# Dealing the first group's weight steps out earlier in a fused retention and feed-forward kernel

## The chip, the cores and the metric

One core of one Trainium2 chip runs the whole kernel. The metric is the device time of one execution in microseconds; the kernel before was run three times, and one further execution was profiled.

## The reference, cut to what matters

Attention with decay (retention) over 4 batches, 8 heads, 576 positions and a head size of 64; then two feed-forward layers over the 2304 tokens of 512 channels, with 2048 hidden units each.

```python
scores = scale * np.matmul(q, k.transpose(0, 1, 3, 2))
ret = scores * Dmat[None, :, :, :]      # gamma_h ** (i - j) for i >= j, else 0
x = np.matmul(ret, v)                   # -> tokens x 512
h = x @ w_in;  x = np.maximum(0.01 * h, h) @ w_out
h = np.maximum(x @ w_in2, 0.0);  x = h * h @ w_out2
```

The weights reach the chip as 64-bit floats, read as pairs of 32-bit words. Products are made of three passes of a high and a low part each, so every weight and every operand is split on the chip into a "hi" and a "lo" tile.

## The kernel before, in words

**Attention stage.** 20 chunks, 0 to 19: five a batch, four of 128 tokens and one of 64. For a chunk i of the loop (L611) the program issues the loads of chunk i + 4 on the SP queue, then `scores` and `decay` of chunk i + 2, then `output` of chunk i. `scores` (L501) is 16 matmuls on PE into one of two wide PSUM tiles, and a product with the mask on DVE into r (L513). So PE can't begin the scores of chunk i + 2 until DVE has made r of chunk i. `decay` (L515) is up to two products on GpSimd (POOL). `output` (L528) is r times v (L539), q times the running state (L542), the sums for the next state (L548) on PE; ACT copies the sums into the state (L554) and the output into ysb (L557). Every engine takes its instructions in the order in which the program issues them.

**Weight steps.** Dealt out between the chunks are two lists of other work. `Weights.steps` is a generator that turns weights into hi and lo tiles, one step each time it is asked. A group of hidden units has four weights, two input weights with 12 steps each (L151) and two output weights with 8 each (L191): 40 steps, of which most are one DVE instruction. Steps 1, 13, 25 and 33 begin a weight with the exponent on ACT (L149). Steps 10, 11, 22 and 23 have the hi copies of input weights on ACT (L185), followed by the lo of DVE (L187). Of an output weight, the first step also holds the shift at L201, and then come L203, L205, L207, L209 on DVE, the hi on ACT (L212), and L214 and L216 on DVE. All weights pass through one tile `raw` and one work tile `sf`. `RATE[i]` says how many steps follow the output of chunk i; `FIRST` runs three before chunk 0; `run` stops at `GROUP - OWN`, 40 less `OWN`; and what is missing to this count is run in one go after the last chunk (L651). When the weight in hand no longer needs `raw`, `next` (L137) sets `free`, and the following chunk issues the next load (L617), up to four loads (`GRP`) in this stage. After the stage a load is issued by `next` itself. A step whose weight has not been asked for yields, and the caller goes on without it.

**Operand builds.** `operands(0, 0)` makes the seven operands x of the first 768 tokens out of ysb, in eleven steps behind chunks 8 to 18 (`BUILD`): hi on ACT (L256), lo on DVE (L260), sums on DVE (L270 to L281). The x tiles are also stored to DRAM by SP (L237) for later groups.

**Feed-forward stage.** Two layers, four groups each, three pairs of token blocks p each. `first` (L334) makes seven products (L318) by Strassen's scheme into two wide PSUM tiles a and b, in the order A11, A12, S2, S3, S1, A22, S4; the first two of the whole stage are issued early, behind chunks 17 and 18 (L639). The sum at L370 reads b, and PE can write S3 into b only after it; the sum at L384 reads a, which S4 then overwrites. `second` (L402) is the products with the output weights (L419). `pace` (L665) asks for weight steps between these, up to a share of the group's 40 that `SHARE` gives by the place reached, at most two a call.

Of the kernel before, what the change touches and what calls it, by code (L numbers as in the profile page):

```python
# [23 lines left out]
GRP = 4  # L24
# [6 lines left out]
HW = DM // 2  # L31
SLOTS = 7
INS, OUTS = 3, 2 * NU
RATE = [1, 2, 2, 2] + [2] * 6 + [1, 1, 2, 2, 2, 0, 0, 0, 1, 2]
BUILD = [0] * 8 + [1] * 11 + [0]
DEEP = 4
SPACE = .65
SHARE = {0: (0.15, 0.45), NG - 1: (0.47, 0.85), NG: (0.2, 0.55)}
OWN = 5
LAG = 1  # L40
ARRIVE = 3
FIRST = 3
# [8 lines left out]
def retention_ffn_kernel(ctx: ExitStack, tc: tile.TileContext, full, rows, half, halfv, w1, w2, const, mask, gk, out):  # L51
# [44 lines left out]
    def weight_tiles(pool, ins, outs):  # L96
        for _ in range(ins):
            i = len(in_tiles)
            in_tiles.append((pool, i))
        for _ in range(outs):  # L100
            i = len(out_tiles)
            out_tiles.append((pool, i))
# [139 lines left out]
    def operands(layer, p):  # L242

        x = ysb[p].rearrange("p (k t n) -> p k t n", k=NK, t=2)
        b11, b21, b12, b22 = (x[:, k : k + 2, t] for t in range(2) for k in (0, 2))
        t2 = stage.tile([P, 2, HT], F32, tag="t2", name="t2")

        xt = {}

        def hi(i, src):  # L250
            use = layer, 0, p, i
            while uses[loaded[0]] != use or loaded[0] == used[0] + SLOTS:
                yield True
            loaded[0] += 1
            xt[i] = xs[use] = xpool.tile([P, 2, 2, HT], F32R, tag="x", name="x")
            nc.scalar.activation(xt[i][:, 0], src, AF.Copy)  # L256

        def lo(i, src):
            t = xt[i]
            nc.vector.tensor_tensor(t[:, 1], src, f32(t[:, 0]), sub)  # L260
            kept.append(((layer, 0, p, i), t))


        yield from hi(0, b11)
        yield
        yield from hi(1, b21)
        lo(0, b11)
        yield
        lo(1, b21)
        nc.vector.tensor_tensor(b11, b12, b11, sub)  # L270
        yield
        nc.vector.tensor_tensor(t2, b22, b11, sub)
        yield
        yield from hi(2, t2)
        nc.vector.tensor_tensor(b12, b22, b12, sub)
        yield
        yield from hi(3, b12)
        lo(2, t2)
        yield
        yield from hi(4, b11)  # L280
        nc.vector.tensor_tensor(b21, b21, t2, sub)  # L281
        yield
        yield from hi(5, b21)
        lo(3, b12)
        yield
        yield from hi(6, b22)
        lo(4, b11)
        yield
        lo(5, b21)
        yield  # L290
        lo(6, b22)
        yield
# [267 lines left out]
    weights = Weights()  # L560
# [5 lines left out]
    def run(n, limit):  # L566

        while n > 0 and done[0] < limit:
            if next(steps, None):
                break  # L570
            done[0] += 1
            n -= 1

    def build(n=1):

        ran = 0
        while builds and ran < n:
            try:
                if next(builds[0]):
                    break  # L580
                ran += 1
            except StopIteration:
                builds.pop(0)
        return ran

    GROUP = NU * (STEPS_IN + STEPS_OUT)
    with tc.manual_schedule():
        with tc.tile_pool(name="att", bufs=1) as pool:
# [22 lines left out]
            for i in range(n):  # L611
# [16 lines left out]
                if a < 2 * HT <= a + t:  # L628
                    builds.append(operands(0, 0))
                run(min(1, RATE[i]), GROUP - OWN)  # L630
                if BUILD[i] > 0:
                    build()
                run(RATE[i] - 1, GROUP - OWN)
                if BUILD[i] > 1:
# [8 lines left out]
                    else:  # L643
                        early.append(sums1)
        att.clear()
        if weights.free and weights.loads < GRP:
            weights.ahead()
        more = ctx.enter_context(tc.tile_pool(name="more", bufs=1))
        gp = ctx.enter_context(tc.tile_pool(name="gp", bufs=1))
        weight_tiles(more, INS - NU, OUTS - NU)  # L650
        run(GROUP, GROUP - OWN)  # L651
        weights.arrive = ARRIVE
# [110 lines left out]
```

## Time and profile before

| | us |
|---|---|
| median of 3 runs | 845.59 |
| lowest and highest | 843.33, 846.24 |
| the profiled execution | 844.29 |
| its span in the trace | 842.5 |
| PE busy in the span | 824.2 (98%) |
| DVE, ACT, POOL busy | 601.4, 340.7, 49.8 |

Rows of the trace give the start of an instruction or of a run of like ones, in us from the start of the span, then the time, the engine, the line and the tiles written and read; in brackets is how long the engine sat idle before it and what released it. The mean granted TensorE clock of the span is 0.993 of full speed.

### The profile page before, as it was taken

Reading aid. Unit: us, or ns where it says so; the run is one execution under the profiler, and the core shown is the slowest. Engines: PE = TensorE matmul, PEld = TensorE weight load, DVE = VectorE, ACT = ScalarE, POOL = GpSimd, SP = SyncE. Lnnn points to the kernel's source line nnn. Section 1 sums busy time; section 2 is a strip of 40 time slices with the busy share of each in tenths; the row PEclk is TensorE's granted clock in tenths of the full one; section 3 lists DMA queues with packets and bytes.
Section 4 is the critical chain, followed back from the end, with each engine's and each line's share of the span. In section 5 each row is a group of like instructions: output and inputs, shape, how many; then the busy total and the mean of one; then the engine's idle time right before and its main releaser. Section 6 shows DMA issues by size and latency. Waiting matters only on the chain.

```text
span 842.5 us, 12378 instructions
## 1 busy us (share of the span) xinstructions
PE 824.2 (98%) x5084; PEld 778.0 (92%) x5084; DVE 601.4 (71%) x734; ACT 340.7 (40%) x447; POOL 49.8 (6%) x36
## 2 busy tenths in 40 slices
PE   6999999999999999999999999999999999999998
PEld 6878899999999999999999998988998998998996
DVE  4799588758667576658667879868777778754534
ACT  1455557545424424424425365543322333321211
POOL 3766000000000000000000000000000000000000
PEclk8999999999999999999999999999999999999999
DMA  9998463967547647646832554966755646735711
GB/s 334 346 311 288 181 241 95 420 264 279 217 190 268 219 150 298 242 147 242 301 112 103 209 226 163 368 255 238 285 183 206 262 160 252 262 133 204 286 52 75
DMA packets 45688, 191.01 MB, mean 227 GB/s; under 512 B 5696, under 2 KB 6720, under 8 KB 45632
## 3 DMA queue, kind: packets, MB, share of 16 engines
q1 hardware_dynamic: 45632, 190.22, 60.7%
q8 instruction: 40, 0.66, 0.3%
q14 instruction: 16, 0.13, 0.0%
HBM read 152.45 MB, written 37.75 MB: 226 GB/s over the span
## 4 chain that ended last, share of the span: by engine, by line
PE 86%; DVE 7%; DMA 4%; ACT 1%; issue 1%; SPq 0%; DVEq 0%; ACTq 0%
PE yps L419 46%; PE a L318 22%; PE b L318 16%; DMA raw<-in_w 1%; DVE r L513 1%; DMA x<-x 1%; DVE x L260 1%; PE scps L511 1%; DMA kt<-in_full 1%; DMA kv<-in_rows 1%; PE ops L539 1%; PE ops L542 1%; DVE sf L205 1%; ACT sf L149 1%; DVE ilo L187 1%
## 5 line engine op out<-in xcount | busy, mean ns | idle before, releaser
L318 PE MATMUL a<-x,ihi 128*128 128x384 f32 x768 | 196.0, 336 | 2.2 <-DVE t L384 2.1
L318 PE MATMUL b<-x,ihi 128*128 128x384 f32 x576 | 147.2, 336 | 2.1 <-DVE t L370 2.1
L318 PEld LDWEIGHTS a<-x,ihi 128*128 128x128 f32 x768 | 138.9, 188 | 4.3 <-DVE t L384 3.4
L419 PE MATMUL yps<-ghi,ohi 128*128 128x384 f32 x384 | 128.6, 335 | 0.6 <-ACT ysb L428 0.6
L318 PE MATMUL a<-x,ilo 128*128 128x384 f32 x384 | 128.6, 335 | 0.0
L419 PE MATMUL yps<-ghi,olo 128*128 128x384 f32 x384 | 128.3, 334 | 0.0
L419 PE MATMUL yps<-glo,ohi 128*128 128x384 f32 x384 | 128.3, 334 | 0.0
L356 DVE TENSOR_TENSOR glo<-t,ghi 128x768 fp32r<-128x768 f32 x96 | 91.7, 955 | 45.8 <-ACT ghi L351 45.3
L430 DVE TENSOR_TENSOR ysb<-yps,ysb 128x384 f32<-128x384 f32 (+1 forms) x126 | 76.0, 610 | 62.6 <-PE yps L419 62.1
L419 PE MATMUL yps<-ohi,glo 128*128 128x512 f32 x288 | 112.3, 390 | 0.0
L419 PE MATMUL yps<-olo,ghi 128*128 128x512 f32 x288 | 112.3, 390 | 0.0
L419 PE MATMUL yps<-ohi,ghi 128*128 128x512 f32 x288 | 112.0, 389 | 0.0
L351 ACT ACTIVATE ghi<-t 128x768 fp32r<-128x768 f32 x96 | 81.1, 845 | 68.5 <-DVE t L329 55.1
L318 PEld LDWEIGHTS b<-x,ihi 128*128 128x128 f32 x576 | 104.3, 189 | 2.6 <-DVE t L370 2.4
L344 ACT ACTIVATE s<-a 128x768 f32<-128x768 f32 x47 | 38.2, 813 | 157.3 <-PE a L318 157.2
L318 PE MATMUL b<-x,ilo 128*128 128x384 f32 x288 | 96.8, 336 | 0.0
L419 PEld LDWEIGHTS yps<-ghi,ohi 128*128 128x128 f32 x384 | 72.1, 188 | 1.5 <-ACT ysb L428 0.9
L318 PEld LDWEIGHTS a<-x,ilo 128*128 128x128 f32 x384 | 72.2, 188 | 0.0
L419 PEld LDWEIGHTS yps<-glo,ohi 128*128 128x128 f32 x384 | 72.1, 188 | 0.0
L419 PEld LDWEIGHTS yps<-ghi,olo 128*128 128x128 f32 x384 | 72.1, 188 | 0.0
L419 PEld LDWEIGHTS yps<-ohi,glo 128*128 128x128 f32 x288 | 54.1, 188 | 11.2
L419 PEld LDWEIGHTS yps<-olo,ghi 128*128 128x128 f32 x288 | 54.1, 188 | 11.0
(67 smaller groups left out, 1002.5 us busy)
## 6 DMA issues: line engine op xcount, KB each, us to landing
x<-x SPq DMA_DIRECT2D x168, 768.0 KB, 6.2
raw<-in_w SPq DMA_DIRECT2D x62, 512.0 KB, 5.1
kv<-in_rows SPq DMA_DIRECT2D x16, 512.0 KB, 6.2
out<-ysb SPq DMA_DIRECT2D x18, 256.0 KB, 2.0
q<-in_full SPq DMA_DIRECT2D x16, 256.0 KB, 5.8
kt<-in_full SPq DMA_DIRECT2D x16, 256.0 KB, 5.6
ysb<-in_w SPq DMA_DIRECT2D x2, 512.0 KB, 7.1
gq<-in_const SPq DMA_DIRECT2D x3, 256.0 KB, 7.3
```

What stands on the lines that cost most here:

```text
L149: nc.scalar.activation(f32(a), f32(raw[:, :, 1]), AF.Abs)
L187: nc.vector.tensor_tensor(lo[:, a:z], sf[:, a + 1 : z + 1], f32(hi[:, a:z]), sub)
L205: nc.vector.scalar_tensor_tensor(rest, high, 23, low, ALU.logical_shift_left, ALU.bitwise_or)
L260: nc.vector.tensor_tensor(t[:, 1], src, f32(t[:, 0]), sub)
L318: nc.tensor.matmul(ps[:, u, :HT], a[:, w, s], x[:, b, k], start=(start and k == 0 and i == 0), stop=(k == 1 and i == 2), skip_group_check= ...
L344: nc.scalar.activation(t, ps[:, :, :HT], AF.Copy)
L351: nc.scalar.activation(h, t, AF.Copy)
L356: nc.vector.tensor_tensor(l, t, f32(gs[key][0]), sub)
L419: nc.tensor.matmul(acc, a, b, start=(j == u == i == 0), stop=(j == 1 and u == NU - 1 and i == 2))
L430: nc.vector.tensor_tensor(y, acc, y, add)
L511: nc.tensor.matmul(ps[:n, j, p, :n], k[s, c], q[s, c], start=True, stop=True)
L513: nc.vector.tensor_tensor(t[:n, :, :, :n], ps[:n, :, :, :n], self.mask[:n, :, :, :n], mul)
```

## The change

The first group's steps are dealt out at another rate: three a chunk from chunk 2 to chunk 7, two a chunk from 8 to 11, one behind chunk 12, none behind chunks 13 to 17, two behind 18 and three behind 19. `OWN` falls from 5 to 2, so that up to 38 of the 40 steps may run in the attention stage. Since `next` of the fourth weight then falls in this stage, the load after it, the next group's first, is issued right behind the last chunk.

```diff
-RATE = [1, 2, 2, 2] + [2] * 6 + [1, 1, 2, 2, 2, 0, 0, 0, 1, 2]
+RATE = [1, 2] + [3] * 6 + [2] * 4 + [1] + [0] * 5 + [2, 3]
 BUILD = [0] * 8 + [1] * 11 + [0]
...
-OWN = 5
+OWN = 2
...
         att.clear()
-        if weights.free and weights.loads < GRP:
+        if weights.free:
             weights.ahead()
```

## Rows read from the trace of the kernel before

**Rows 1.** Windows: busy us of PE, PEld, DVE, ACT, POOL; clock, DMA share, GB/s.

```profile
36.00:60.00 24.00, 23.00 (x362) 20.24 (x358) 22.45 (x21) 12.87 (x25) 17.53 (x14) 1.00 0.89 308
93.00:97.00 4.00, 4.00 (x16) 4.00 (x15) 2.49 (x4) 3.56 (x5) 0.00 (x0) 0.57 0.37 113
```

**Rows 2.** Waits of PE, 17 to 92 us: total us, times, longest.

```profile
PE scps L511 <- DVE r L513: 2.2, 4, 0.9
```

**Rows 3.** Timeline of PE: start us, us, line, tiles, count, idle before, releaser.

```profile
59.09 1.16 PE L542 MATMUL ops<-q,state 128*128 128x128 f32 x8
...
61.72 1.16 PE L511 MATMUL scps<-q,kt 64*128 64x128 f32 x16 [0.86 <-DVE r L513]
...
71.27 1.16 PE L511 MATMUL scps<-q,kt 64*128 64x128 f32 x16 [0.33 <-DVE r L513]
...
74.25 1.13 PE L542 MATMUL ops<-q,state 128*128 128x128 f32 x8 [0.80 <-POOL kv L526]
...
79.26 0.62 PE L318 MATMUL a<-x,ihi 128*128 128x384 f32 x2
...
92.50 0.61 PE L318 MATMUL b<-x,ihi 128*128 128x384 f32 x2 [2.08 <-DVE t L370]
...
132.77 0.61 PE L318 MATMUL a<-x,ihi 128*128 128x384 f32 x2 [0.98 <-DVE t L384]
```

**Rows 4.** Chain of waits, 92 to 101 us: start us, us, engine, tile, line.

```profile
92.50 3.53 PE b L318 x12
96.04 2.46 PE a L318 x12
98.50 2.08 PE b L318 x12
```

**Rows 5.** Timeline of DVE, columns as in rows 3.

```profile
30.29 0.41 DVE L179 TENSOR_TENSOR sf<-sf 128x256 f32<-128x256 f32 x1
32.09 1.23 DVE L513 TENSOR_TENSOR r<-scps,mask 128x1024 f32<-128x1024 f32 x1 [1.39 <-PE scps L511]
33.23 1.05 DVE L187 TENSOR_TENSOR ilo<-sf,ihi 128x768 fp32r<-128x768 f32 x1
35.08 1.23 DVE L187 TENSOR_TENSOR ilo<-sf,ihi 128x1024 fp32r<-128x1024 f32 x1 [0.80 <-ACT ihi L185]
...
38.85 1.38 DVE L159 TENSOR_SCALAR sf<-sf 128x1024 f32<-128x1024 f32 x1 [1.41 <-ACT sf L149]
...
49.11 1.38 DVE L175 TENSOR_TENSOR sf<-sf 128x256 f32<-128x256 f32 x1
...
56.19 1.21 DVE L513 TENSOR_TENSOR r<-scps,mask 128x1024 f32<-128x1024 f32 x1
57.32 0.94 DVE L187 TENSOR_TENSOR ilo<-sf,ihi 128x768 fp32r<-128x768 f32 x1
...
61.59 1.21 DVE L187 TENSOR_TENSOR ilo<-sf,ihi 128x1024 fp32r<-128x1024 f32 x1
...
64.20 0.67 DVE L201 TENSOR_SCALAR raw<-raw 128x1024 uint32<-128x1024 uint32 x1
...
67.40 1.20 DVE L205 SCALAR_TENSOR_TENSOR sf<-raw 128x1024 uint32<-128x1024 uint32 x1
...
70.00 1.21 DVE L513 TENSOR_TENSOR r<-scps,mask 128x1024 f32<-128x1024 f32 x1
```

**Rows 6.** Timeline of ACT, columns as in rows 3.

```profile
88.60 1.12 ACT L149 ACTIVATE sf<-raw 128x1024 f32<-128x1024 f32 x1
...
104.82 1.57 ACT L256 ACTIVATE x<-ysb 128x768 fp32r<-128x768 f32 x2
```

**Rows 7.** DMA issues (KB each, median us to landing); then SP's timeline.

```profile
x<-x SPq DMA_DIRECT2D x168, 768.0 KB, 6.2
...
kt<-in_full SPq DMA_DIRECT2D x16, 256.0 KB, 5.6
...
72.40 0.81 SPq L132 DMA_DIRECT2D raw<-in_w  x2
```

## The prediction

> **What bounds the kernel now.** I went from the windows to PE's waits, then to what DVE, ACT and POOL did under them. Chunks are counted 0 to 19; the first group's weight steps 1 to 40 (1 to 12 and 13 to 24 for the two input weights, 25 to 32 and 33 to 40 for the third and fourth, which are output weights). The attention stage ends where the first early product starts on PE, at 79.26 us [rows 3]; until then DVE and PE are both nearly full [rows 1], and what PE waits for is mostly the masked scores r that DVE makes: 2.2 us in four waits [rows 2], two of them in [rows 3], with one more of 0.80 at 74.25. The profile books that one to POOL, but the code gives L542 the state, which ACT copies right behind the hi of step 30 (L212), itself waiting for DVE's L209; I take it as the price of an ACT step that waits for DVE ahead of the state copy. Then comes the largest single wait of PE, 2.08 us before the product at 92.50, for the sum at L370. Its cause stands on ACT: the fourth weights' exponent (L149, step 33) starts only at 88.60, behind the last chunk's copies [rows 6], and L203, L205 and L370 queue behind it on DVE. After that wait PE is granted 0.57 of its clock [rows 1], so it spends most of that stretch at the lower of its two levels, 1.2 GHz: two products of twelve matmuls take 3.53 and 2.46 where the next takes 2.08 [rows 4], so the clock costs 1.45 + 0.38 = 1.83 us more. Behind it PE runs to the end with few waits, so what moves PE here by some us moves the end by as much.
>
> **What the edit does, counted.** Before, 4 steps are run by the end of chunk 0, 6 by chunk 1, then two a chunk: 22 by chunk 9, 28 by chunk 13, 33 by chunk 19 and 35 before the feed-forward stage. After, 9 by chunk 2, 12, 15, 18, 21, 24 by chunk 7, then 26, 28, 30, 32, and 33 by chunk 12; none until chunk 18 runs two and chunk 19 three: 38. By this count step 33, the exponent that starts late, runs in chunk 12, and five steps, not six, lie behind the last two chunks. Up to chunk 1 nothing changes; from the second pair of products of the feed-forward stage on (p = 1) the steps are asked for by the same table, so only the time between changes. The work in all is the same.
>
> **Gain at L370.** With step 33 done in chunk 12, L207 and L209 are all that precedes L370 after the last chunk and they wait for no ACT instruction; the sum's inputs are there while PE is busy with S2. So the 2.08 goes. With PE unbroken I expect no fall of the clock, which takes the 1.83 too: -3.91 us. Bounds: at most that; at the least 2.08 minus what is late next, which is the hi of step 38 (L212) at the place on ACT where L149 stood, with nothing on DVE ahead of L370 behind it.
>
> **Loss before it: r of chunk 12.** r(12) is queued on DVE behind the steps of all chunks up to 9: 22 before, 28 after. The six added are L187 twice, L201, L203, L205, L207: 0.94 + 1.21 + 0.67 + 0.67 + 1.20 + 0.67 = 5.36 [rows 5] (L201 stands there for L203 and L207, of the same kind and shape), less about 0.07 each, by which one starts ahead of the former's end (56.19 + 1.21 against 57.32): 4.94 us. Against it stands idle time of DVE that they fill: 1.39 + 0.80 + 1.41 = 3.60 before [rows 5]. Not all of it can be used: steps 11 and 12 now stand in chunk 3 ahead of r(6), and step 11 needs ACT's hi, which needs chunk 3's copies. DVE is done by 30.29 + 0.41 less the overlap, 30.63, and the lo at L187 starts no sooner than its row, 33.23: 2.60 us of idle, with r(6) stuck behind it and the second lo until about 35.3 instead of 32.09. So 1.0 us is regained, and r(12) starts at 56.19 + 4.94 - 1.0 = 60.1.
>
> From there to the end of the stage: step 29 (L209) and step 30 (L212) now follow r(12), as they follow the r at 70.00 before, and from that r's start to the L542 that waited for the state copy the rows give 74.25 - 70.00 = 4.25. From chunk 12's L542 (59.09) to the early product (79.26) PE took 20.17, of which 0.86 + 0.33 + 0.80 were waits [rows 3]: 18.18 unbroken. Behind chunk 12 DVE has hardly a step left, so I let those waits go. The early product starts at 60.1 + 4.25 + 18.18 = 82.5: **+3.3 us**. Bounds: below, PE cannot do better than without its waits, 2.2 + 0.8 = 3.0 us sooner; above, every added step can meet a POOL instruction as the L175 at 49.11 did, 1.38 against 0.41 for an instruction of that shape [rows 5], 0.97 each: 6 x 0.97 = 5.8 more, +9.1. I take +3.3 since POOL has the same instructions as before.
>
> That price rests on a collision which the rows show for instructions with two SBUF inputs and not for r, 1.21 at 56.19 as at 70.00. [...]
>
> **Smaller terms.** Steps 39 and 40 and five of the next group's, which ran behind the first products' matmuls at L419, now fall among the first seven products, and L384 is queued behind L161 and L163. PE waited 0.98 for an L384 so placed at 132.77 [rows 3]. Between 0 and 1.0 I take 0.5.
> On SP the second output weight's load moves from chunk 15 to chunk 11 and has the loads of chunks 16 to 19 behind it; it waits for step 29. That ends about 60.1 + 2 x 1.13 = 62.4, after which kt of chunk 16 is issued near 63.7 and lands 5.6 later [rows 7], 69.3. PE wants it 5.6 us of matmuls after L542(12), at about 70: covered by 0.7 us, and a rival below if not. The third weight's load moves two chunks up and is covered by chunk 7's work. The next group's first load moves ahead of the six stores of x on SP and waits for step 37. Their slots are written again from 104.82 [rows 6]; 1 MB and six times 768 KB [rows 7] at 308 GB/s [rows 1] take about 18.5 us from about 88, and the slots come up one by one, the first after 6 us: nothing.
>
> **Sum.** -3.91 + 3.3 + 0.5 = -0.1 us. The profiled execution took 844.29 us, its span 842.5 and 1.8 around it, so 844.2; it stands 1.3 below the median of the runs shown, 845.59, on which the sum gives **845.5**. 0.3% is 2.5 us, about what a measurement can tell from no change.
>
> **Rivals**, by where r(12) starts (each us later is a us at the end):
> 1. *The early steps stay hidden.* If collisions become fewer since the steps spread over more of POOL's idle time, and r(12) starts by 57.7, the stage loses under 0.9 and the net is below -2.5. At the floor, 3.0 sooner: -3.91 - 3.0 + 0.5 = -6.4, 839.2; midway 841. For it: DVE idles 3.60 in [rows 5], and DVE has slack again from chunk 13. Against: the order on DVE puts two of the steps on an ACT round trip. 27%.
> 2. *Collisions multiply (slower).* Denser steps meet POOL in chunks 4 to 9, and r(12) starts after 62.8, a net above +2.5. Three more of 0.97 give 848.4; all six 851.3. It would also lengthen PE's single waits, and one near 2 us could lower the clock again, as at 92.50. For it: POOL is busy 17.53 of the 24 us [rows 1]. Against: POOL's count is unchanged. 20%.
> 3. *Chunk 16's kt is late (slower).* The load on SP that waits for step 29 keeps it. The 1 MB ahead of it at 308 GB/s is 3.4 us, less the 0.7 of cover: up to 2.7, so 848.2. No such wait is in the rows, where the attention loads are all issued before the second output weight's, at 72.40 [rows 7]. 4%.
> 4. *The steps don't move*, because a load is not yet asked for and the generator yields: then the catch-up run in front of the feed-forward stage takes them, and the time stays 845.6. The count above speaks against it. 3%.
> The forecast itself has 46%, its own range 843 to 848.
>
> **Numbers.** Faster by over 0.3%: 27%, rival 1. Slower: 20 + 4 = 24%. Within: 46 + 3 = 49%. The range, 840.5 to 849.5, takes most of rival 1 and all but the dense end of rival 2.
>
> **What would show it.** Right: no PE wait at L370 and a granted clock near 1.00 behind S2; the first early product 2 to 5 us after 79.26; PE waits for r of chunks 6 to 12 and one before chunk 12's L542; none from chunk 13 on. The first step: r(6) near 35.3 instead of 32.09. The second: r(12) near 60. Wrong: an early product at or ahead of 79.26 (rival 1), one behind 85 or short matmuls at the lower clock in that stage (rival 2), a PE wait for a DMA of kt (rival 3), or a difference behind 160 us, which no step here explains.

## The result: slower by 0.57%, and the profile after

The changed kernel took **849.03 us** (median of 5 runs, 848.18 to 850.09), the kernel before 844.27 (5 runs beside them): a ratio of 1.0057, 95% interval 1.0040 to 1.0073. The forecast was 845.5, no change to be told. The range, 840.5 to 849.5, held the time, but that is partly luck: it was built on the 845.59 of the three runs shown. On 844.27 the forecast change of -0.1 gives 844.2 and the same range ends at 848.2, below what was measured. The likeliest case and its chance were wrong: rival 2, which had 20%, came true. The profiled execution took 848.18 us, the lowest of the five, with a span of 846.4, 3.9 more than that of before; the medians are 4.8 apart. PE is busy as long as before (824.3 us against 824.2): in sum, what was added is waiting.

(PE is the matrix engine, DVE the vector engine, ACT the scalar engine, POOL is GpSimd, and SP issues the loads.)

The windows of the changed kernel, for the stretches of [rows 1] (busy us of PE, PEld, DVE, ACT and POOL, then clock, DMA share, GB/s):

```profile
36.00:60.00 24.00, 20.36 (x304) 17.86 (x302) 22.75 (x23) 12.49 (x23) 13.68 (x10) 0.93 0.78 267
93.00:97.00 4.00, 4.00 (x39) 3.68 (x38) 1.34 (x2) 1.75 (x3) 0.00 (x0) 1.00 0.90 296
```

From 36 to 60 us PE now works 20.36 us instead of 23.00 and its clock is at 0.93; around the old wait at L370 it is full and at 1.00. So the loss lies ahead of the early products and the gain behind. The waits of PE from 17 to 110 us, against [rows 2], show with whom:

```profile
PE scps L511 <- DVE r L513: 6.2, 5, 2.0
PE ops L542 <- ACT state L554: 1.3, 1, 1.3
PE a L318 <- DVE t L384: 0.7, 1, 0.7
```

6.2 us for r instead of 2.2. The timeline of PE, with the columns and places of [rows 3]:

```profile
38.01 1.16 PE L511 MATMUL scps<-q,kt 64*128 64x128 f32 x16 [1.18 <-DVE r L513]
...
42.38 0.68 PE L511 MATMUL scps<-q,kt 64*64 64x64 f32 x16 [0.48 <-DVE r L513]
...
47.77 1.16 PE L511 MATMUL scps<-q,kt 64*128 64x128 f32 x16 [1.98 <-DVE r L513]
48.86 1.62 PE L539 MATMUL ops<-r,kv 128*64 128x128 f32 x16
50.41 2.08 PE L542 MATMUL ops<-q,state 128*128 128x128 f32 x8
...
64.28 0.68 PE L511 MATMUL scps<-q,kt 64*64 64x64 f32 x16 [1.93 <-DVE r L513]
...
67.26 1.13 PE L542 MATMUL ops<-q,state 128*128 128x128 f32 x8 [1.27 <-ACT state L554]
...
69.67 1.16 PE L511 MATMUL scps<-q,kt 64*128 64x128 f32 x16 [0.67 <-DVE r L513]
...
86.18 0.62 PE L318 MATMUL a<-x,ihi 128*128 128x384 f32 x2
...
97.19 0.51 PE L318 MATMUL b<-x,ihi 128*128 128x384 f32 x2
...
104.33 0.62 PE L318 MATMUL a<-x,ihi 128*128 128x384 f32 x2 [0.73 <-DVE t L384]
...
106.55 0.33 PE L419 MATMUL yps<-ghi,ohi 128*128 128x384 f32 x1
```

The early product starts at 86.18 instead of 79.26. Behind the wait of 1.98 us two runs of matmuls take 1.62 and 2.08 instead of their usual 1.09 and 1.16: the lower clock (0.56 is granted from 48.86 to 52.42), where the kernel before was granted 1.00 from 36 to 60 [rows 1]. The wait at L370 is gone (S3 goes on at 97.19 without a gap), and there is one of 0.73 at L384.

The timeline of DVE, which answers to [rows 5]:

```profile
24.40 1.23 DVE L513 TENSOR_TENSOR r<-scps,mask 128x1024 f32<-128x1024 f32 x1 [1.47 <-PE scps L511]
...
33.78 3.04 DVE L187 TENSOR_TENSOR ilo<-sf,ihi 128x768 fp32r<-128x768 f32 x2 [1.68 <-ACT ihi L185]
36.74 1.21 DVE L513 TENSOR_TENSOR r<-scps,mask 128x1024 f32<-128x1024 f32 x1
...
44.63 1.95 DVE L168 SCALAR_TENSOR_TENSOR sf<-raw,sf 128x1024 f32<-128x1024 uint32 x1
...
55.78 0.69 DVE L203 TENSOR_SCALAR sf<-sf 128x1024 f32<-128x1024 f32 x1 [1.01 <-ACT sf L149]
...
57.52 2.17 DVE L205 SCALAR_TENSOR_TENSOR sf<-raw 128x1024 uint32<-128x1024 uint32 x1
59.62 1.79 DVE L260 TENSOR_TENSOR x<-ysb,x 128x768 fp32r<-128x768 f32 x1
...
61.33 1.76 DVE L207 TENSOR_SCALAR sf<-sf 128x1024 uint32<-128x1024 uint32 x1
63.01 1.21 DVE L513 TENSOR_TENSOR r<-scps,mask 128x1024 f32<-128x1024 f32 x1
```

r of chunk 6 is at 36.74 instead of 32.09, r of chunk 12 at 63.01 instead of 56.19. L205, L260 and L207, which take 1.22, 0.95 and 0.69 us where GpSimd's products are left out (below), take 2.17, 1.79 and 1.76.

One thing has to be taken off before the sum: the r of chunk 3, the last one ahead of anything the change moves, starts at 24.40, in the kernel before at 23.84:

```profile
23.84 1.23 DVE L513 TENSOR_TENSOR r<-scps,mask 128x1024 f32<-128x1024 f32 x1 [1.70 <-PE scps L511]
...
102.50 0.33 PE L419 MATMUL yps<-ghi,ohi 128*128 128x384 f32 x1
```

These 0.56 us belong to the start of that one execution: over all sixteen profiles of this document the r of chunk 3 starts anywhere from 22.48 to 25.92, with either table. The rest, by places:

| us, from the trace | before | after | difference |
|---|---|---|---|
| r of chunk 3 | 23.84 | 24.40 | +0.56, not of the change |
| from there to r of chunk 12 | 32.35 | 38.61 | +6.26 |
| from there to the early product | 23.07 | 23.17 | +0.10 |
| from there to the first L419 | 23.24 | 20.37 | -2.87 |
| from there to the end of the span | 740.00 | 739.85 | -0.15 |
| span | 842.5 | 846.4 | +3.9 |

The first L419 is the second line above. From there on the two kernels are alike. The stretch from r of chunk 3 to r of chunk 12 hardly varies: it is 38.59 to 38.87 us in the five profiles below and above that have the new table up to chunk 11 and GpSimd's products, and 32.35 to 32.60 in the eight that have the old one. So the +6.26 is the change's, not one execution's.

### The profile page after: what moved, and what is told of

It is laid out like the page before. It is cut to its first block, busy times and chain, and to the rows that moved or that the text cites. A ratio compares the mean times of both kernels' runs of the same rounds, so it can differ in the third digit from the quotient of the medians.

```text
span 846.4 us, 12380 instructions
## 1 busy us (share of the span) xinstructions
PE 824.3 (97%) x5084; PEld 777.6 (92%) x5084; DVE 604.9 (71%) x734; ACT 340.2 (40%) x447; POOL 47.5 (6%) x36
## 4 chain that ended last, share of the span: by engine, by line
PE 88%; DVE 5%; DMA 4%; ACT 2%; issue 1%; SPq 0%; DVEq 0%; ACTq 0%
PE yps L419 46%; PE a L318 22%; PE b L318 16%; DMA kt<-in_full 2%; PE ops L542 1%; PE ops L539 1%; PE scps L511 1%; DMA raw<-in_w 1%; DMA kv<-in_rows 1%; ACT sf L149 1%; DVE ilo L187 1%; PE sums L548 1%; DVE r L513 1%; DVE sf L205 1%; DVE t L370 0%
## 5 line engine op out<-in xcount | busy, mean ns | idle before, releaser
L419 PE MATMUL yps<-ghi,ohi 128*128 128x384 f32 x384 | 128.6, 335 | 0.5 <-ACT ysb L428 0.4
L419 PE MATMUL yps<-ghi,olo 128*128 128x384 f32 x384 | 128.3, 334 | 0.0
L419 PE MATMUL yps<-glo,ohi 128*128 128x384 f32 x384 | 128.3, 334 | 0.0
L419 PE MATMUL yps<-ohi,glo 128*128 128x512 f32 x288 | 112.3, 390 | 0.0
L419 PE MATMUL yps<-olo,ghi 128*128 128x512 f32 x288 | 112.2, 390 | 0.0
L419 PE MATMUL yps<-ohi,ghi 128*128 128x512 f32 x288 | 112.0, 389 | 0.0
L344 ACT ACTIVATE s<-a 128x768 f32<-128x768 f32 x47 | 38.3, 814 | 157.0 <-PE a L318 156.9
L419 PEld LDWEIGHTS yps<-ghi,ohi 128*128 128x128 f32 x384 | 72.1, 188 | 1.4 <-ACT ysb L428 0.8
L419 PEld LDWEIGHTS yps<-glo,ohi 128*128 128x128 f32 x384 | 72.1, 188 | 0.0
L419 PEld LDWEIGHTS yps<-ghi,olo 128*128 128x128 f32 x384 | 72.1, 188 | 0.0
L370 DVE TENSOR_TENSOR t<-b,s 128x768 f32<-128x768 f32 x24 | 23.0, 957 | 61.8 <-PE b L318 57.2
L419 PEld LDWEIGHTS yps<-ohi,glo 128*128 128x128 f32 x288 | 54.0, 188 | 11.3
```

What stands on the lines that cost most here:

```text
L344: nc.scalar.activation(t, ps[:, :, :HT], AF.Copy)
L370: nc.vector.tensor_tensor(t11, b[:, :, :HT], s1, add)
L419: nc.tensor.matmul(acc, a, b, start=(j == u == i == 0), stop=(j == 1 and u == NU - 1 and i == 2))
```

## Experiments

Times are medians. "Before" stands for the kernel before, run beside each of them: 844.2 to 844.4 us.

**Loss and gain taken apart.** First the late half alone, then the early half alone.

```diff
# late half alone, on the changed kernel
-RATE = [1, 2] + [3] * 6 + [2] * 4 + [1] + [0] * 5 + [2, 3]
+RATE = [1, 2, 2, 2] + [2] * 6 + [1, 1, 2, 2, 2, 1, 1, 1, 2, 3]
# early half alone, on the kernel before (OWN = 5)
-RATE = [1, 2, 2, 2] + [2] * 6 + [1, 1, 2, 2, 2, 0, 0, 0, 1, 2]
+RATE = [1, 2] + [3] * 6 + [2] * 4 + [0] * 7 + [1]
```

> The changed kernel's OWN of 2 and early load, but the five steps added to the kernel before's table stand behind chunks 15 to 19 instead of 2 to 12. Theory (the loss is the steps put ahead of r in chunks 2 to 9, the gain is step 33 off the end): the early product starts within 1 us of the 79.26 of before, no wait at L370, 2.08 + 1.83 gained less about 0.7 at L384: 841 us. Rival (the wait at L370 vanished only because PE came 7 us later): the wait is still there and the time is that of before, 844.3.

> The changed kernel's table up to chunk 11, but step 33 behind the last chunk and OWN of 5, as before. Theory (loss and gain are separate): the early product near 86, as in the changed kernel, and the wait of about 2 us at L370 with the lower clock behind it back again: 844.3 + 6.9 = 851 us. Rival (the late PE hides that wait anyway): 849, as the changed kernel.

The early half alone came out near the theory: 850.52 us (four executions), ratio 1.0065 (1.0044 to 1.0087). That is above the whole change, but the intervals overlap; the trace decides. Its early product starts at 87.43, and the wait at L370 is back:

```profile
100.66 0.62 PE L318 MATMUL b<-x,ihi 128*128 128x384 f32 x2 [2.08 <-DVE t L370]
```

The lower clock that I expected behind it did not come back. The window from 100.60 to 106.00 us, with the columns of [rows 1]:

```profile
100.60:106.00 5.40, 5.34 (x31) 5.34 (x31) 3.88 (x6) 3.92 (x5) 0.00 (x0) 1.00 0.46 127
```

So the loss sits in the early steps, and the gain at L370 is separate from it. The late half alone missed: 845.5 us, ratio 1.0014 (1.0000 to 1.0027), where I expected 841. Its executions fall into two groups, 843 to 845 and 846 to 848, and the profiled one, 847.59, is of the upper: there PE waits 2.85 us for the r of chunk 16, ahead of which the steps are those of the kernel before, and 1.26 at L384, where ACT waits 0.69 for the early load. The wait of 2.85, and the last of the three DVE instructions ahead of that r:

```profile
75.19 2.08 PE L511 MATMUL scps<-q,kt 64*128 64x128 f32 x16 [2.85 <-DVE r L513]
...
72.26 1.75 DVE L207 TENSOR_SCALAR sf<-sf 128x1024 uint32<-128x1024 uint32 x1
```

and GpSimd at the same place in the kernel before:

```profile
66.85 4.37 POOL L522 TENSOR_TENSOR q<-q,gq 128x512 f32<-128x512 f32 x1 [5.41 <-PE scps L511]
```

In the kernel before L205, L260 and L207 run there in 1.20, 0.94 and 0.68 us and GpSimd's product is the one that gets longer; here they take 1.52, 1.79 and 1.75. It is the same meeting, and the other engine loses it. What decides that, and whether it is what makes the two groups, was not settled. That the late half has a cost of its own is followed up below.

**GpSimd's part.** Its decay products were taken out of both kernels.

```diff
     def decay(self, i):
         q, _, kv = self.raw[i]
...
-            if c > 0:
-                q = q[:, : NP * n].rearrange("p (a t) -> p a t", t=n)
-                nc.gpsimd.tensor_tensor(q, q, self.gq[c - 1], mul)
-            if c < FULL:
-                k = kv[:, 0, :].rearrange("p (h e) -> p h e", e=D)
-                g = self.gk[:, c].unsqueeze(2).to_broadcast([P, H, D])
-                nc.gpsimd.tensor_tensor(k, k, g, mul)
```

> The changed kernel without the decay products on GpSimd (that part of the computation is left out; q and k stay unscaled). Theory (collisions with GpSimd made r of chunk 12 late by 2.9 us more than forecast): without them r of chunk 12 starts at 55 to 57 instead of 63, and the early product near 78 to 80 instead of 86. Rival (the order and the round trips through ACT alone make r late): r of chunk 12 no earlier than 60, the early product at 83 or later.

> The kernel before without the decay products on GpSimd (the same part left out). Theory: DVE is ahead of PE throughout, r of chunk 12 starts at 51 to 53 and the early product at 76 to 77, PE's floor; the changed kernel without GpSimd stands 2 to 3 us behind it instead of 6.9. Rival: the two stand as far apart as with GpSimd.

The changed kernel is no longer the slower one: it takes 838.99 us (two executions, 837.80 and 840.19), the kernel before 841.37 (four, 840.08 to 841.85). Whether it is the faster one, so few executions do not tell. The r of chunks 3 and 12 on DVE, first of the changed kernel without the products:

```profile
23.18 1.23 DVE L513 TENSOR_TENSOR r<-scps,mask 128x1024 f32<-128x1024 f32 x1 [1.73 <-PE scps L511]
...
54.29 1.22 DVE L513 TENSOR_TENSOR r<-scps,mask 128x1024 f32<-128x1024 f32 x1
```

and of the kernel before without them:

```profile
23.83 1.23 DVE L513 TENSOR_TENSOR r<-scps,mask 128x1024 f32<-128x1024 f32 x1 [2.13 <-PE scps L511]
...
51.12 1.22 DVE L513 TENSOR_TENSOR r<-scps,mask 128x1024 f32<-128x1024 f32 x1
```

From r of chunk 3 to r of chunk 12 it is 31.11 against 27.29 us. The difference is 3.82, and the forecast's ledger of steps, 4.94 less 1.0, had said 3.94. With GpSimd it is 38.61 against 32.35. So the meetings with GpSimd cost 7.50 us in the changed kernel and 5.06 in the one before.

That these are in the main longer instructions and not longer waits is seen in DVE's busy time over the same stretches. It is 35.60 us in the changed kernel with GpSimd's products and 26.93 without, 8.67 more; in the kernel before 28.54 and 22.16, 6.38 more. DVE runs 24 instructions there besides the r's in the changed kernel, 18 in the kernel before: 0.36 and 0.35 us more for each. The six added steps pay on average what the others pay. The extra cost arises early, as the r of chunk 8 shows, in the changed kernel, in the kernel before, and in the two without GpSimd's products in the same order:

```profile
46.50 1.21 DVE L513 TENSOR_TENSOR r<-scps,mask 128x1024 f32<-128x1024 f32 x1
40.15 1.21 DVE L513 TENSOR_TENSOR r<-scps,mask 128x1024 f32<-128x1024 f32 x1
41.57 1.22 DVE L513 TENSOR_TENSOR r<-scps,mask 128x1024 f32<-128x1024 f32 x1
39.44 1.22 DVE L513 TENSOR_TENSOR r<-scps,mask 128x1024 f32<-128x1024 f32 x1
```

| what GpSimd's products add, us | before | changed |
|---|---|---|
| from r of chunk 3 to r of chunk 8 | 0.70 | 3.71 |
| from there to r of chunk 12 | 4.36 | 3.79 |

The early product of the changed kernel and of the kernel before, both without GpSimd's products:

```profile
77.94 0.62 PE L318 MATMUL a<-x,ihi 128*128 128x384 f32 x2
76.83 0.62 PE L318 MATMUL a<-x,ihi 128*128 128x384 f32 x2
```

From the same r of chunk 3 it is 54.76 and 53.00 us off: 1.8 apart, where the full kernels are 6.4 apart. The rivals' numbers for both runs did not come; my own were a little high for the changed kernel (r of chunk 12 at 55 to 57, the early product at 78 to 80). The early table by itself costs little: without GpSimd half of its 3.8 us is regained before the early product.

Then only the half with q was taken out of the changed kernel (the first three lines removed above):

> The changed kernel with only the k half of GpSimd's decay products (the q products are left out). Theory (r of chunk 12 is late by the collisions, 63.0 with all and 54.3 with none of GpSimd's products): about half of it, 57 to 60.5, and an early product between 79 and 84. Rival (a few of the meetings carry it all): 63 or 54.

841.48 us, the r of chunk 3 at 23.23 and

```profile
55.51 1.21 DVE L513 TENSOR_TENSOR r<-scps,mask 128x1024 f32<-128x1024 f32 x1
```

that is 32.28 us from r to r: the k products alone cost 1.17 us, where both cost 7.50. I expected half, and the rival's 54 is nearer; the price is not in proportion. With both products a chunk, GpSimd has the next one queued when the first ends, and may come in again between two DVE steps. But the k products alone also start at other times, most of them when their own load lands. Which of the two makes them so cheap was not tested.

**The gain at L370 by itself.** Two tables on the kernel before, OWN and loads untouched:

```diff
-RATE = [1, 2, 2, 2] + [2] * 6 + [1, 1, 2, 2, 2, 0, 0, 0, 1, 2]
# step 31 behind chunk 17, 32 and 33 behind 18
+RATE = [1, 2, 2, 2] + [2] * 6 + [1, 1, 2, 2, 2, 0, 0, 1, 2, 2]
# steps 31 to 33 behind chunk 18
+RATE = [1, 2, 2, 2] + [2] * 6 + [1, 1, 2, 2, 2, 0, 0, 0, 3, 2]
```

> The kernel before with one step of its table moved: step 31 behind chunk 17, steps 32 and 33 (the exponent) behind chunk 18, so that only L203 and L205 follow the last chunk. OWN and the loads as before. Theory (the whole gain is the exponent off the last chunk's copies, 2.08 + 1.83): no wait at L370, 844.3 - 3.9 = 840.4 us. Rival (the stage end moves as much, by collisions of the two moved DVE steps with GpSimd): 844.

> As the run with the exponent behind chunk 18, but all three steps 31 to 33 behind chunk 18, where GpSimd's last product is nearly over. Theory: no wait at L370 and no step added where GpSimd works: the early product as in the kernel before, 840.4 us, and at or below the run that puts step 31 behind chunk 17. Rival (collisions there cost nothing): both the same.

840.79 us, ratio 0.9964 (0.9951 to 0.9977), and 840.71 us, ratio 0.9963 (0.9947 to 0.9980): 3.6 and 3.7 us below before, 3.9 expected. No wait at L370 and none of the lower clock. They are alike, so the place of step 31 makes no difference that can be told, as the second rival had it. In the second, the early product starts at 78.71 and the first L419 at 98.29, 19.58 us later instead of 23.24: the forecast's -3.91 for this term measured -3.66.

The kernel before was also run again:

> The kernel before once more, for a second profile. Theory (who holds the SBUF port at a meeting of DVE and GpSimd depends on small shifts): the early product's start differs from 79.26 by some us between executions, with the waits for r at other chunks, and the time spreads over 842 to 848. Rival (the stage is steady): 79.3 within 0.5, and the two groups of times in the first late-only run come from its own change.

844.19 us. Its early product starts at 78.69, with the waits of [rows 3] to within 0.02 us and r of chunk 3 as much earlier (23.25) as the product; my expectation of a stage that shifts by some us was wrong for this kernel, though its twelve runs spread over 843.05 to 846.78.

**The late half.** With the table of before, and four steps behind each of the last two chunks:

```diff
# on the changed kernel (OWN = 2)
+RATE = [1, 2, 2, 2] + [2] * 6 + [1, 1, 2, 2, 2, 0, 0, 0, 4, 4]
# the same with OWN = 3
+RATE = [1, 2, 2, 2] + [2] * 6 + [1, 1, 2, 2, 2, 0, 0, 0, 4, 3]
```

> The kernel before's table up to chunk 17, then four steps behind each of the last two chunks, with OWN of 2 and the next group's load early, as in the changed kernel. Theory: the stage end as before, no wait at L370, 0.7 to 1.3 at L384 as in the changed kernel: 841.1 to 841.7 us, some 0.7 to 1.3 above the run with OWN of 5. Rival (the late half of the change costs by itself, through the load or the steps among the first products): 844 or more.

> As the run with four steps behind each of the last two chunks, but three behind the last and OWN of 3: step 38, and with it the next group's load, falls after the stage, so step 41 may not start before its time. Theory (the 5.8 us between that run and the one with OWN of 5 are step 41's exponent waiting on ACT for a load that has only just been issued): no wait of ACT for a DMA, no wait of PE at S1, 840.8 to 841.5 us. Rival (too many steps behind the last two chunks hold up L370): 843 or more, with the wait of 1.1 at L370 and the low clock behind it.

With OWN of 2: 846.49 us, ratio 1.0036 (1.0023 to 1.0049), 5.8 above the table with OWN of 5, and the rival's case. PE waits twice:

```profile
91.21 0.62 PE L318 MATMUL b<-x,ihi 128*128 128x384 f32 x2 [1.11 <-DVE t L370]
...
98.96 0.62 PE L318 MATMUL b<-x,ihi 128*128 128x384 f32 x2 [3.31 <-ACT s L344]
```

and the second wait is ACT's, on its timeline:

```profile
97.08 1.12 ACT L149 ACTIVATE sf<-raw 128x1024 f32<-128x1024 f32 x1 [3.54 <-DMA raw<-in_w]
98.10 0.81 ACT L344 ACTIVATE s<-b 128x768 f32<-128x768 f32 x1
```

Step 41's exponent (L149) is next on ACT and waits for the load of its weight; the copy at L344, which A22 needs, stands behind it. The load can be issued only when step 37 has done with `raw`, here at about 90.3 us. With OWN of 3 the wait of 3.31 is gone, and the time is 842.86 us, ratio 0.9992 (0.9975 to 1.0009), nearer the rival's 843 than the theory's 841. There is a wait of 1.10 at L370, as the rival had it but without the lower clock, since L207 and L209 now stand ahead of it behind an exponent that ran only behind chunk 18. So both causes are there. By the medians they are 3.6 us (the load) and 2.1 us (the crowding at L370), but the second rests on twelve executions from 840.4 to 847.8, of which the profiled one is the lowest. By the traces, from the early product to the first L419 the table with OWN of 5 takes 19.58 us, OWN of 3 takes 21.20, OWN of 2 takes 26.07: 1.6 for the crowding and 4.9 for the load, with the lower clock behind the wait of 3.31 in it (0.60 is granted from 98.90 to 103.00).

Does this cost stand in the changed kernel too? There the same variant:

```diff
-RATE = [1, 2] + [3] * 6 + [2] * 4 + [1] + [0] * 5 + [2, 3]
+RATE = [1, 2] + [3] * 6 + [2] * 4 + [1] + [0] * 5 + [2, 2]
-OWN = 2
+OWN = 3
```

> The changed kernel with two steps instead of three behind the last chunk and OWN of 3: the next group's load and step 41 fall where they did before. Theory (in the changed kernel PE comes 7 us late, so the load lands in time and only the 0.73 at L384 is lost by the late half): 848.3 us. Rival (the late half costs the 5.8 us there too): 843 to 844.

> The changed kernel again, side by side with its variant with OWN of 3. Theory (the late half costs the 0.73 at L384 and nothing else; the 2.8 us between the medians of the two in separate runs is the spread of the stage from one execution to the next): 848 to 849 and within 1.5 us of the other. Rival (the late half costs about 2.8 us, in some executions through ACT's wait for the load): 2.3 or more above the other, and in a second profile a wait of ACT for that load.

> The changed kernel with OWN of 3 again. Theory: 847 to 848, within 1.5 us of the changed kernel beside it, its early product near 86 and no wait at L384 in the first pair. Rival: 846 or less, 2.3 or more below it.

The first run gave 846.22 us, between theory and rival. Side by side the changed kernel took 848.47 and the variant 847.36, 1.1 apart, and in neither profile does ACT wait for the load: in the changed kernel the load is issued at 90.96 and step 41 begins at 98.83, by itself. The wait at L384 is 0.73 in both profiles of the changed kernel and absent in both of the variant. So PE's lateness covers the load, and the late half costs about 1 us there: from the early product to the first L419 the changed kernel takes 20.37 and 20.34 us in its two profiles, the variant 19.31 in both of its. The 2.8 us between the separate runs I put down to the spread between executions, which is not shown by itself: the second profile of the changed kernel took 849.86 us, its early product at 87.45, with r of chunk 3 already 1.5 later than in the first.

**A wait that the page books to GpSimd, and the best table.** Step 30 was moved from chunk 14 to chunk 15, behind that chunk's state copies, on top of steps 31 to 33 behind chunk 18:

```diff
-RATE = [1, 2, 2, 2] + [2] * 6 + [1, 1, 2, 2, 2, 0, 0, 0, 1, 2]
+RATE = [1, 2, 2, 2] + [2] * 6 + [1, 1, 2, 2, 1, 1, 0, 0, 3, 2]
```

> The run with steps 31 to 33 behind chunk 18, and step 30 (the hi of L212) moved from chunk 14 to behind chunk 15, that is behind that chunk's state copies on ACT. Theory (the 0.80 before chunk 16's L542 is the state copy queued behind L212): that wait goes, the early product 0.8 sooner, 839.9 us. Rival (it is GpSimd's product, as the profile has it): the wait stays, 840.7.

839.43 us, ratio 0.9944 (0.9928 to 0.9960): the lowest of the kernels that leave nothing out, though its interval overlaps that of the run it builds on. On ACT and PE of that kernel

```profile
71.14 0.78 ACT L554 ACTIVATE state<-sums 64x256 f32<-64x256 f32 x2 [1.53 <-PE sums L548]
...
72.48 1.06 ACT L212 ACTIVATE ohi<-sf 128x1024 fp32r<-128x1024 f32 x1
```

```profile
72.46 1.09 PE L539 MATMUL ops<-r,kv 128*64 128x128 f32 x16
73.48 1.16 PE L542 MATMUL ops<-q,state 128*128 128x128 f32 x8
```

the state copy comes first, L212 after it, and L542 of chunk 16 follows without the 0.80 that stands at 74.25 in [rows 3]. The product of GpSimd to which the page had booked the wait is still there, and it runs on past the start of that L542, until 74.22:

```profile
71.28 2.94 POOL L526 TENSOR_TENSOR kv<-kv,gk 128x512 f32<-128x512 f32 x1
```

So L542 did not wait for it. From r of chunk 3 to the early product it is 54.84 us instead of the 55.44 of the run with step 30 at chunk 14: of the 0.8, 0.6 arrives there.

## Why the prediction failed, by its own steps

- **The count of the steps** held: 33 by chunk 12, five behind the last two chunks. The timeline of DVE has them so. Only the "not six" compares with nothing: in the kernel before it is five there, too (steps 31 to 35).
- **The gain at L370**, -3.91: right in its cause and nearly in size, -3.66 where only that was changed. Its second part, 1.83 for the clock, is less certain than the first. Both profiles of the kernel before have the lower clock behind that wait (0.57 granted); the early half alone and the kernel before without GpSimd's products have the wait, 2.08 and 2.07, and 1.00 granted behind it.
- **The ledger to r of chunk 12** (4.94 of steps, 1.0 us of idle time regained): right where GpSimd's products are out, 3.82 us measured for 3.94.
- **The step that failed** is the sentence "I take +3.3 since POOL has the same instructions as before". It prices the six added steps at their bare length and their meetings with GpSimd at nothing. But the added steps met GpSimd's products as the others do, at 0.36 us each on average. Up to r of chunk 12 the meetings cost 7.50 us, not the 5.06 of the kernel before: 2.4 us more, and of these 2.3 are longer DVE instructions (8.67 less 6.38). In the 7.50 is 1.0 us of waiting at L203 (55.78) that the meetings bring about indirectly: PE waits 1.98 for a late r, runs chunk 8's output at the lower clock, and ACT's exponent stands behind that output's copies. The term was bounded at +9.1, and 6.36 lies inside; the value taken from inside the bounds was wrong.
- **Which instructions meet.** The prediction took the collision to be one of instructions with two SBUF inputs. That is too narrow: L207, with one SBUF input, took 1.76 us, and in [rows 5] L159 took 1.38; both take 0.69 without GpSimd's products. r, with one input in SBUF and one in PSUM, takes 1.20 to 1.23 in all sixteen profiles. The Trainium skill (SBUF — State Buffer, Who interferes with whom) lets a DVE instruction with at most one SBUF input go free only outside the modes that use both ports, and names tensor_scalar among those that can enter them. These traces agree: L207 and L159 are tensor_scalar instructions, r is not.
- **From r of chunk 12 to the early product**, 4.25 + 18.18 = 22.43: 23.17. L542 follows r by exactly 4.25 (67.26 less 63.01), with the state copy behind L212 as its last wait, but one more wait for r, 0.67 at 69.67, stood where I let all go: ahead of the r of chunk 13 stand two operand builds, L260 and L270, which take 1.49 and 1.79 us (0.95 each without GpSimd's products). In all the stage lost 6.36 us where I had 3.3: 2.3 by r and 0.7 here.
- **"With PE unbroken I expect no fall of the clock"** held for S2 and S3. I left the lower clock inside the stage to rival 2, and it came there, behind the wait of 1.98.
- **L384**, +0.5 of 0 to 1.0: 0.73.
- **The load on SP that waits for step 29**, covered by 0.7 us: the trace has no wait of PE for it, so rival 3 did not come, but the cover was used up. The chain of waits of the changed kernel has kt of chunk 16 in it:

```profile
66.75 6.82 DMA kt<-in_full
73.57 0.14 issue
73.70 1.16 PE scps L511 x16
```

- **The next group's early load**, "nothing": true only because PE came late. Where the stage ended on time it cost 3.6 us by the medians. I had asked when the stores behind it would land, not which ACT instruction would wait for the load itself.
- **The sum**: 6.36 - 2.87 is +3.5 for what I gave as +3.3 - 3.91 + 0.5 = -0.1; with 0.56 of the start and -0.15 of the rest that is the span's 3.9. The second profile of the changed kernel has 38.59, 22.94 and 20.34 us in the three middle rows of the table, so the sum holds for it, too. Why the medians differ by 4.8 and these two spans by 3.9 is not shown beyond the spread of the start.

## What to carry to other kernels

When steps are moved earlier into a stretch where two engines lengthen each other's instructions, price each added step at the length that its neighbours have there, not at its bare one: the same work of the other engine cost half as much again here. To take late work off the end, move that work alone, not the whole table (one digit of it gave 3.7 us here), and of a load that is issued earlier, ask which engine that works in order reaches its first reader sooner than it lands.

## What the runs showed of the hardware that I had not expected

The price of GpSimd's products on DVE is far from proportional to their number: with all of them it is 7.50 us up to r of chunk 12, with the k products alone 1.17. To the number of DVE's instructions it is nearly proportional in the two tables, 0.35 and 0.36 us for each one besides the r's. At one and the same meeting either engine can be the one that is lengthened: GpSimd's product in the kernel before (4.37 us), three of DVE's instructions in the profile of the late half alone.

And a wait of 1.98 us for one r, in a stretch of small matmuls, was enough to show the lower clock behind it (1.62 and 2.08 for runs that take 1.09 and 1.16), while in the same execution one of 1.93 at 64.28 was not followed by it: the run of L539 at 64.89 took its 1.09. The profile of the same kernel taken a second time has 1.97 for the run of L539 at 66.48, behind a wait of 1.95 at 65.77, so whether such a wait is followed by the lower clock differs from one execution to the next. At L370 it is the same: a wait of 2.08 us was followed by 0.57 granted in the kernel before and by 1.00 in the early half alone.
